# Numerators in three steps over successive slots, another order of the first MLP's first units, and a new spread of the weights' preparation

## The chip, the cores and the metric

The kernel runs on one core of one Trainium2 chip. The metric is the device time of one execution in microseconds. A core has PE (TensorE, matrix products into the PSUM accumulator), VectorE (DVE), ScalarE (ACT), GpSimd (POOL), and SP, which here only issues DMAs. Every engine works through its own queue in program order; the kernel writes that order out by hand, and the engines wait for each other by semaphores.

## The reference

```python
def phi(x):
    proj = np.einsum('bhsd,df->bhsf', x, w_phi)
    proj = proj - np.max(np.abs(proj), axis=-1, keepdims=True)
    return np.concatenate([np.exp(proj), np.exp(-proj)], axis=-1)
q_p, k_p = (phi(q), phi(k))                     # batch 2, heads 8, seq 576, head_dim 64
kv = np.einsum('bhsf,bhsd->bhfd', k_p, v)
z = np.sum(k_p, axis=2)
num = np.einsum('bhsf,bhfd->bhsd', q_p, kv)
den = np.einsum('bhsf,bhf->bhs', q_p, z)[..., None] + 1e-06
x = num / den                                    # as (1152, 512)
...
x = (x @ w_a) * (x @ w_b) @ w_out                # first MLP, d_ff 1536
...
p = domain_probs / (domain_probs.sum(-1, keepdims=True) + 1e-09)
for e in range(4):                               # second MLP, four experts
    out += p[:, e:e + 1] * (np.maximum(x @ w1[e], 0.0) @ w2[e])
```

## The kernel before, in words

**Slots.** Attention runs in slots. Each of 36 items (18 for keys, 18 for queries, `NK = 18`, `NI = 36`) is two tiles of 128 rows of a pair of heads. Slot s projects item s (`pj`: six matmuls, L165 to L167); VectorE takes the row maximum `mx` (L170) and the difference `r` (L172). For a key item ScalarE makes the two exponentials, and three slots later PE adds up `kv`. For a query item PE transposes `r` four slots later (`rt`, L219), and ScalarE writes the exponentials into `qp` (L237). The input of an item is split into a high and a low part three slots ahead, by ScalarE (`xp`, L84) and GpSimd (L85). `pj` and `rt` share four PSUM buffers (pool `u`), so PE can be at most about two slots ahead of VectorE's `r` and ScalarE's `qp`.

**Numerators.** After 4.5 query slots half of a batch's heads is complete, and `num` is called one slot later (for the last half two slots later). `stage_num` issues 48 matmuls on tiles of 32 columns, in three groups of 16 into the two `nd` buffers of PSUM: the denominators (copied out by ScalarE as `den`), then the two halves of the numerator. The third group takes the buffer of the first. In the next slot VectorE makes the reciprocals (`dt`, `rc`, `dt`, `rb`), and in that and the one after multiplies (`x`, L289); a slot after each `x`, `stage_xparts` splits it into `xh` (ScalarE, L295) and `xl` (GpSimd, L296), which the first MLP reads.

**First MLP.** `unit_ab(j, tp)` is for column blocks 2j and 2j+1 (f = 0, 1) and batch `tp`: eight products of 12 matmuls (L608 to L610), four per f, alternating between the a half and the b half of the weights. The product of both, `gg`, is split into `hhb` by ScalarE and VectorE. Eight output products `o1` of six matmuls (L638 to L640) are queued for later; `free_hh(tp)` flushes those that still have to read the part of `hhb` that is about to be written. The first eight products, unit (0, 0), are given out in the last slots (`FILL`), the others by `run`, in the order of the list `order`.

**Preparation of the weights.** Weights arrive as 64-bit numbers in halves (list `f64`: ("ab", 0) with halves 0 and 1, ("ab", 1) with 2 and 3, ("o", 0) with 4 and 5, ("ab", 2) with 6 and 7, ("ab", 3) with 8 and 9, and so on). Each goes through three steps:

```python
def begin(k):   # ScalarE: m (L361), rn (L362)
def middle(k):  # VectorE: m, m, wx (L369, L372, L375); GpSimd: wx (L378); then load_raw() of half k + 2 on SP
def parts(k):   # ScalarE: w (L84); GpSimd: w (L85)
...
for k in range(NW + 2):   # the order of the steps
    if k >= 2: ...parts(k - 2)
    if 1 <= k <= NW: ...middle(k - 1)
    if k < NW: ...begin(k)
```

`prep(n)` does the next n steps; in `run` 1.4 of them fall due after each product, and `need(u)` does at once what a unit still lacks. Half 0 of a block is the a half, half 1 the b half, so the second product of a unit is the first to read the second half. Raw halves of "ab" come in eight DMAs on SP's queue, which also carries the loads of keys, queries (`xraw`) and `v`.

Of the kernel before, what the change touches and what calls it, by code (L numbers as in the profile page):

```python
# [9 lines left out]
F32 = mybir.dt.float32  # L10
F32R = mybir.dt.float32r
U32 = mybir.dt.uint32
AF = mybir.ActivationFunctionType
# [3 lines left out]
B, H, S, D = 2, 8, 576, 64  # L17
# [9 lines left out]
HT = S // 2  # L27
FP1 = FA // 2
# [19 lines left out]
def tile_linear_attention_then_mlps(ctx, tc, qT, kT, v, w_phi, wab, wout, w12, probs, out):  # L48
    nc = tc.nc
# [15 lines left out]
    nd_p = tc.alloc_tile_pool(name="nd", bufs=2, space=PSUM)  # L65
    xt_p = None
    q_p = None
# [6 lines left out]
    with tc.manual_schedule():  # L74
# [80 lines left out]
        kvz_t = {}  # L155
        qp_t = {}
# [56 lines left out]
        def stage_rt(i):  # L213
            kind, b, g, ts_ = items[i]
            r = st_r[i]
            ps = u_p.tile([128, 2, 2, 128], F32, tag="u", name="rt")
            for j in range(2):
                for h in range(2):
                    nc.tensor.transpose(out=ps[:, h, j, :], in_=r[:, 2 * j + h, :], identity=ident)  # L219
            for t in ts_:  # L220
                for p in ([t[0]] if t[0] != "m" else t[1:]):
                    if (b, p) not in qp_t:
                        qp_t[b, p] = q_p.tile([128, 2, 2, S], F32, tag="qp", name="qp", bufs=3)
            done = []
            spans = []
            if ts_[0][0] != "m" and ts_[1][0] == ts_[0][0]:
                spans.append((ts_[0][0], ts_[0][1] * 128, ps.rearrange("p h t s -> p h (t s)"), 256))
            else:
                for j, t in enumerate(ts_):
                    if t[0] == "m":  # L230
                        for m in range(2):
                            spans.append((t[1 + m], 512, ps[:, :, j, 64 * m:64 * m + 64], 64))
                    else:
                        spans.append((t[0], t[1] * 128, ps[:, :, j, :], 128))
            for p, c, src, n in spans:
                for s in range(2):
                    nc.scalar.activation(  # L237
                        out=qp_t[b, p][:, s, :, c:c + n], in_=src, func=AF.Exp, scale=1.0 - 2.0 * s
                    )
            for t in ts_:  # L240
                if t[0] == "m":
                    done.append((b, t[1]))
                elif t[0] % 2 == 1 and t[1] == 3:
                    done.append((b, t[0]))
            return done
# [4 lines left out]
        tt = {}  # L250
        xc = {}

        def stage_num(b, half):
            pairs = [(b, 2 * half + k) for k in range(2)]
            qp = [qp_t.pop(bp) for bp in pairs]
            den = q_p.tile([128, 2, HT], F32, tag="den", name="den", bufs=1)
            x = []
            for k in range(3):
                t = nd_p.tile([128, 2, 512], F32, tag="nd", name="num")
                for i in range(2):  # L260
                    for s in range(2):
                        for n in range(4):
                            h = n % 2
                            c = 64 * (1 - h) if k == 0 else 64 * h + 32 * (k - 1)
                            nc.tensor.matmul(  # L265
                                out=t[32 * n:32 * n + 32, i, 0:HT],
                                lhsT=kvz_t[pairs[n // 2]][:, h, s, c:c + 32],
                                rhs=qp[n // 2][:, s, h, HT * i:HT * i + HT],
                                start=(s == 0), stop=(s == 1), tile_position=(0, 32 * n),
                            )  # L270
                if k == 0:
                    nc.scalar.activation(out=den, in_=t[:, :, 0:HT], func=AF.Copy, bias=1e-6)
                else:
                    x.append(t)
            return x, den

        def stage_rc(den):
            dt = q_p.tile([128, 18, 32], F32, tag="dt", name="dt", bufs=1)
            nc.vector.transpose(out=dt.rearrange("p a b -> p (a b)"), in_=den.rearrange("p a b -> p (a b)"))
            rc = q_p.tile([128, 18, 1], F32, tag="rc", name="rc", bufs=2)  # L280
            nc.vector.reciprocal(out=rc, in_=dt[:, :, 0:1])
            nc.vector.tensor_copy(dt, rc.to_broadcast([128, 18, 32]))
            rb = q_p.tile([128, 2, HT], F32, tag="rb", name="rb", bufs=1)
            nc.vector.transpose(out=rb.rearrange("p a b -> p (a b)"), in_=dt.rearrange("p a b -> p (a b)"))
            return rb

        def stage_x(t, rb):
            x = q_p.tile([128, 2, HT], F32, tag="x", name="x", bufs=2)
            nc.vector.tensor_tensor(out=x, in0=t[:, :, 0:HT], in1=rb, op=ALU.mult)  # L289
            return x  # L290
# [192 lines left out]
        def prep(n):  # L483

            while n > 0 and t_next[0] < len(tasks):
                u, fn, writes = tasks[t_next[0]]
                w = ("load",) + u if writes == "load" else u
                if writes and w in before and uses[before[w]] or t_next[0] >= mark and l_p is None:
                    return
                fn()  # L490
                t_next[0] += 1
                n -= 1
# [8 lines left out]
        pos = [0]  # L501
# [207 lines left out]
        def run(gen, rate, tasks_per):  # L709
# [24 lines left out]
            out=wbp[:, 1], in0=wb.rearrange("p h f -> p (h f)"), in1=wbp[:, 0].bitcast(F32), op=ALU.subtract  # L734
# [14 lines left out]
        NI = len(items)  # L749
        NK = NI // 2  # L750
        todo = {}

        def later(slot, fn, *a):
            todo.setdefault(slot, []).append((fn, a))

        def num(slot, b, half):
            later(slot + 1, div, slot + 1, b, half, *stage_num(b, half))

        def div(slot, b, half, x, den):
            rb = stage_rc(den)  # L760
            for k in range(2):
                later(slot + 1 + k, scaled, slot + 1 + k, b, 2 * half + k, x[k], rb)

        def scaled(slot, b, c, t, rb):
            later(slot + 1, stage_xparts, b, c, stage_x(t, rb))


        FILL = [NI + 4, NI + 6, NI + 7, NI + 8]
        fill = unit_ab(0, 0)

        for slot in range(NI + 10):
            if slot < NI:
                kind, b, g, ts_ = items[slot]
                if slot + 3 < NI:
                    split_x(slot + 3, nc.gpsimd)
                stage_proj(slot)
            if slot == NK + 4:
                for fn, a in todo.pop(slot, []):
                    fn(*a)
                k_p.release()  # L780
                xt_p = tc.alloc_tile_pool(name="xt", bufs=1, side="left", reuse_waits="tile")
                for bb in range(B):
                    xh[bb], xl[bb] = (xt_p.tile([128, KD, S], F32R, tag=f"x{bb}{n}", name="x" + n) for n in "hl")
                q_p = tc.alloc_tile_pool(name="q", bufs=1, side="left", reuse_waits="tile")
            i = slot - 3
            if 0 <= i < NK:
                stage_kv(i)
            i = slot - 4
            if NK <= i < NI:
                for bb, p in stage_rt(i):  # L790
                    if p % 2:
                        n = slot + (2 if i == NI - 1 else 1)
                        later(n, num, n, bb, p // 2)
            for fn, a in todo.pop(slot, []):
                fn(*a)
            if slot == 2:
                for _ in range(2):
                    load_raw()
            if 4 <= slot < 9:
                load_v(1, slot - 4)  # L800
            if slot == 16:
                probabilities()
            if slot in FILL:
                for _ in range(2):
                    next(fill)
                    pos[0] += 1
            if slot in (10, 14):
                prep(3)
            if slot >= NK + 2:
                prep(1)  # L810
        assert not todo
        q_p.release()
        r_p.release()
# [3 lines left out]
        acc_p = ctx.enter_context(tc.tile_pool(name="acc", bufs=4, space=PSUM, reuse_waits="tile"))  # L817


        order = [(j, tp) for j in range(FP1 - 2) for tp in range(B)]  # L820
        order += [(FP1 - 2, 0), (FP1 - 1, 0), (FP1 - 2, 1), None, (FP1 - 1, 1)]
        for jt in order:
            if jt is None:
# [2 lines left out]
            j, tp = jt  # L826
# [63 lines left out]
```

## Time and profile before

| | |
|---|---|
| median of 3 runs | 735.85 us (735.56 to 736.63) |
| the profiled execution | 734.41 us, span 732.6 us |
| PE busy | 711.3 us (97%) |
| VectorE, ScalarE, GpSimd busy | 419.3, 304.2, 302.9 us (57%, 42%, 41%) |
| attention's slots | about 124 us of the span |

A busy PE need not be one at its peak: the records of matmuls overlap, and short gaps hide under their ends. The granted clock of PE is a share of full speed; 1.00 is 2.4 GHz.

### The profile page before, as it was taken

The numbers are of one execution on the slowest core, as the hardware profiler recorded it, in microseconds if no ns is written. First come the engines' busy times: TensorE is split into PE (matmuls) and PEld (weight loads), VectorE is DVE, ScalarE is ACT, GpSimd is POOL, SyncE is SP. The second block draws the span as 40 slices with busy tenths as digits, with TensorE's granted clock in tenths as the row PEclk, the third lists the DMA queues.
The fourth block names the chain that finished last, engine by engine and source line by source line (L and its number), as shares of the span: only waits on it lengthen the run. The fifth ranks groups of instructions, "written<-read, shape, count | busy, mean of one in ns | idle before, by whom it ended". The sixth has DMA issues, their size and how long they took to land.

```text
span 732.6 us, 12645 instructions
## 1 busy us (share of the span) xinstructions
PE 711.3 (97%) x4928; PEld 652.1 (89%) x4928; DVE 419.3 (57%) x717; ACT 304.2 (42%) x626; POOL 302.9 (41%) x277
## 2 busy tenths in 40 slices
PE   7998988999999999999899999999999999999998
PEld 7996657999999999999888898988988898989896
DVE  6678796446666575363545555545455545545454
ACT  6566764554535351243553333323233323333221
POOL 3356545444434354312683425344442535343300
PEclk9999999999999999999999999999999999999999
DMA  7534211222323231022041011111111011100003
GB/s 200 148 111 125 58 59 59 82 92 87 91 83 87 78 96 30 1 58 86 2 116 30 30 57 58 30 55 33 58 40 47 30 59 58 30 29 1 1 1 129
DMA packets 49707, 46.25 MB, mean 63 GB/s; under 512 B 8304, under 2 KB 41584, under 8 KB 49648
## 3 DMA queue, kind: packets, MB, share of 16 engines
q1 hardware_dynamic: 49344, 45.26, 21.0%
q8 instruction: 38, 0.62, 0.4%
q10 hardware_dynamic: 304, 0.20, 0.1%
q14 instruction: 21, 0.17, 0.1%
HBM read 43.08 MB, written 2.36 MB: 62 GB/s over the span
## 4 chain that ended last, share of the span: by engine, by line
PE 92%; DVE 3%; ACT 3%; issue 1%; POOL 1%; DMA 0%; DVEq 0%; ACTq 0%; POOLq 0%
PE acc L682 9%; PE acc L681 9%; PE acc L680 9%; PE ab L609 7%; PE ab L610 7%; PE ab L608 7%; PE X L533 5%; PE kv L199 5%; PE X L534 5%; PE X L535 5%; PE acc L639 3%; PE acc L640 3%; PE acc L638 3%; PE num L265 3%; PE Z L534 2%; PE Z L533 2%
## 5 line engine op out<-in xcount | busy, mean ns | idle before, releaser
L696 DVE SCALAR_TENSOR_TENSOR oacc<-acc,pr,oacc 128x512 f32<-128x512 f32 (+1 forms) x136 | 101.4, 746 | 117.2 <-PE acc L682 117.2
L85 POOL TENSOR_TENSOR w<-wx,w 128x512 fp32r<-128x512 f32 x68 | 92.1, 1355 | 154.9 <-ACT w L84 154.9
L609 PE MATMUL ab<-xl,w 128*128 128x288 f32 x384 | 113.3, 295 | 2.0 <-POOL xl L296 2.0
L85 POOL TENSOR_TENSOR wc<-wt,wc 128x512 fp32r<-128x512 f32 (+1 forms) x48 | 69.8, 1483 | 109.4 <-ACT wc L84 109.4
L682 PE MATMUL acc<-w,hhb 128*128 128x512 f32 x288 | 114.1, 396 | 0.9 <-DVE hhb L657 0.9
L608 PE MATMUL ab<-xh,w 128*128 128x288 f32 x384 | 113.5, 296 | 1.2 <-ACT xh L295 1.2
L610 PE MATMUL ab<-xh,w 128*128 128x288 f32 x384 | 113.4, 295 | 0.0
L681 PE MATMUL acc<-w,hhb 128*128 128x512 f32 x288 | 113.1, 393 | 0.0
L680 PE MATMUL acc<-w,hhb 128*128 128x512 f32 x288 | 112.6, 391 | 0.0
L533 PE MATMUL X<-xc,wc 128*128 128x288 f32 x256 | 77.2, 302 | 1.4 <-ACT h L538 1.4
L534 PE MATMUL X<-xc,wc 128*128 128x288 f32 x256 | 75.8, 296 | 0.7 <-DVE xc L85 0.7
L656 ACT ACTIVATE hhb<-h 128x288 fp32r<-128x288 f32 x64 | 36.2, 566 | 96.8 <-DVE h L541 96.7
L535 PE MATMUL X<-xc,wc 128*128 128x288 f32 x256 | 75.4, 295 | 0.0
L609 PEld LDWEIGHTS ab<-xl,w 128*128 128x128 f32 x384 | 72.2, 188 | 2.2 <-POOL xl L296 2.2
L608 PEld LDWEIGHTS ab<-xh,w 128*128 128x128 f32 x384 | 72.2, 188 | 1.9 <-ACT xh L295 1.5
L378 POOL TENSOR_TENSOR wx<-wx,rn 128x512 uint32<-128x512 uint32 x36 | 46.3, 1287 | 63.1 <-DVE wx L375 63.1
L610 PEld LDWEIGHTS ab<-xh,w 128*128 128x128 f32 x384 | 72.2, 188 | 0.0
L538 ACT ACTIVATE h<-X 128x288 f32<-128x288 f32 x64 | 25.9, 405 | 104.5 <-PE X L535 104.5
L682 PEld LDWEIGHTS acc<-w,hhb 128*128 128x128 f32 x288 | 54.0, 188 | 15.6 <-DVE hhb L657 4.4
L657 DVE SCALAR_TENSOR_TENSOR hhb<-h,hhb 128x288 fp32r<-128x288 f32 x64 | 40.5, 633 | 42.2 <-ACT hhb L656 42.2
L681 PEld LDWEIGHTS acc<-w,hhb 128*128 128x128 f32 x288 | 54.0, 188 | 8.4
L680 PEld LDWEIGHTS acc<-w,hhb 128*128 128x128 f32 x288 | 54.1, 188 | 7.7
(99 smaller groups left out, 1605.8 us busy)
## 6 DMA issues: line engine op xcount, KB each, us to landing
raw<-in_wab SPq DMA_DIRECT2D x192, 64.0 KB, 2.0
wt<-in_w SPq DMA_DIRECT2D x64, 128.0 KB, 2.4
wx<-in_w SPq DMA_DIRECT2D x32, 256.0 KB, 2.9
raw<-in_wout SPq DMA_DIRECT2D x12, 512.0 KB, 3.7
xraw<-in_qT SPq DMA_DIRECT2D x6, 384.0 KB, 3.1
out<-oacc SPq DMA_DIRECT2D x8, 256.0 KB, 2.0
xraw<-in_kT SPq DMA_DIRECT2D x5, 384.0 KB, 4.2
v<-in_v SPq DMA_DIRECT2D x8, 192.0 KB, 4.4
```

The source lines that it names most:

```text
L85: eng.tensor_tensor(out=lo, in0=src, in1=hi.bitcast(F32), op=ALU.subtract)
L378: nc.gpsimd.tensor_tensor(out=x, in0=x, in1=r, op=ALU.add)
L533: nc.tensor.matmul(out=ps, lhsT=whi, rhs=xhi, start=first and a == 0, stop=False, skip_group_check=True)
L534: nc.tensor.matmul(out=ps, lhsT=whi, rhs=xlo, start=False, stop=False, skip_group_check=True)
L535: nc.tensor.matmul(out=ps, lhsT=wlo, rhs=xhi, start=False, stop=a == 1, skip_group_check=True)
L608: nc.tensor.matmul(out=t, lhsT=whi, rhs=hi, start=(c == 0), stop=False)
L609: nc.tensor.matmul(out=t, lhsT=whi, rhs=lo, start=False, stop=False)
L610: nc.tensor.matmul(out=t, lhsT=wlo, rhs=hi, start=False, stop=(c == KD - 1))
L680: nc.tensor.matmul(out=acc, lhsT=hi, rhs=w[:, 0, f], start=f == 0, stop=False)
L681: nc.tensor.matmul(out=acc, lhsT=hi, rhs=w[:, 1, f], start=False, stop=False)
L682: nc.tensor.matmul(out=acc, lhsT=lo, rhs=w[:, 0, f], start=False, stop=f == 1)
L696: nc.vector.scalar_tensor_tensor(out=oc, in0=acc[:, c:c + step], scalar=sc, in1=oc, op0=ALU.mult, op1=ALU.add)
```

## The change

Four things are changed. (1) The numerators are issued in three steps of 16 matmuls in successive slots: denominators (`num`), first half together with the reciprocals (`first`), second half together with the first multiplication (`second`); the second multiplication follows (`third`). The last half is no longer put off by a slot, the loop has one slot less, and `qp` has four buffers. (2) `FILL` gives the eight products of unit (0, 0) out over six slots, from slot 38 on. (3) `PREP` says in which slots a preparation step is made: one in each of the slots 5 to 16, one in 22, 26, 30, 34, one in each of 36 to 44; before, three in slot 10, three in 14, one in each slot from 20 on. (4) Unit (1, 0) goes ahead of (0, 1).

```diff
-                        qp_t[b, p] = q_p.tile([128, 2, 2, S], F32, tag="qp", name="qp", bufs=3)
+                        qp_t[b, p] = q_p.tile([128, 2, 2, S], F32, tag="qp", name="qp", bufs=4)
...
         def num(slot, b, half):
-            later(slot + 1, div, slot + 1, b, half, *stage_num(b, half))
-
-        def div(slot, b, half, x, den):
+            pairs = [(b, 2 * half + k) for k in range(2)]
+            qp = [qp_t.pop(bp) for bp in pairs]
+            kvz = [kvz_t[bp] for bp in pairs]
+            den = stage_den(stage_num(qp, kvz, 0))
+            later(slot + 1, first, slot + 1, b, half, qp, kvz, den)
+
+        def first(slot, b, half, qp, kvz, den):
+            t = stage_num(qp, kvz, 1)
             rb = stage_rc(den)
-            for k in range(2):
-                later(slot + 1 + k, scaled, slot + 1 + k, b, 2 * half + k, x[k], rb)
-
-        def scaled(slot, b, c, t, rb):
-            later(slot + 1, stage_xparts, b, c, stage_x(t, rb))
-
-
-        FILL = [NI + 4, NI + 6, NI + 7, NI + 8]
+            later(slot + 1, second, slot + 1, b, half, qp, kvz, rb, t)
+
+        def second(slot, b, half, qp, kvz, rb, t0):
+            t1 = stage_num(qp, kvz, 2)
+            later(slot + 1, stage_xparts, b, 2 * half, stage_x(t0, rb))
+            later(slot + 1, third, slot + 1, b, half, rb, t1)
+
+        def third(slot, b, half, rb, t1):
+            later(slot + 1, stage_xparts, b, 2 * half + 1, stage_x(t1, rb))
+
+
+        FILL = {NI + 2: 1, NI + 3: 1, NI + 4: 1, NI + 6: 2, NI + 7: 1, NI + 8: 2}
+        PREP = {s: 1 for s in range(5, NK - 1)} | {s: 1 for s in range(NK + 4, NI, 4)} | {s: 1 for s in range(NI, NI + 9)}
...
-                        n = slot + (2 if i == NI - 1 else 1)
-                        later(n, num, n, bb, p // 2)
+                        later(slot + 1, num, slot + 1, bb, p // 2)
...
-            if slot in FILL:
-                for _ in range(2):
-                    next(fill)
-                    pos[0] += 1
-            if slot in (10, 14):
-                prep(3)
-            if slot >= NK + 2:
-                prep(1)
+            for _ in range(FILL.get(slot, 0)):
+                next(fill)
+                pos[0] += 1
+            prep(PREP.get(slot, 0))
...
-        order = [(j, tp) for j in range(FP1 - 2) for tp in range(B)]
+        order = [(0, 0), (1, 0), (0, 1), (1, 1)] + [(j, tp) for j in range(2, FP1 - 2) for tp in range(B)]
```

PE's order in the query slots, at the first numerators (slots 27 and 28). Before:

```order
L219 MATMUL rt<-ident,r 128x128 x4
L265 MATMUL num<-qp,kvz 32x288 x48
L165 MATMUL pj<-wbp,xp 128x256
L166 MATMUL pj<-wbp,xp 128x256
L167 MATMUL pj<-wbp,xp 128x256
L165 MATMUL pj<-wbp,xp 128x256
L166 MATMUL pj<-wbp,xp 128x256
L167 MATMUL pj<-wbp,xp 128x256
L219 MATMUL rt<-ident,r 128x128 x4
```

And of the change:

```order
L219 MATMUL rt<-ident,r 128x128 x4
L260 MATMUL num<-qp,kvz 32x288 x16
L165 MATMUL pj<-wbp,xp 128x256
L166 MATMUL pj<-wbp,xp 128x256
L167 MATMUL pj<-wbp,xp 128x256
L165 MATMUL pj<-wbp,xp 128x256
L166 MATMUL pj<-wbp,xp 128x256
L167 MATMUL pj<-wbp,xp 128x256
L219 MATMUL rt<-ident,r 128x128 x4
L260 MATMUL num<-qp,kvz 32x288 x16
```

The 48 matmuls that stood together are now 16 in this slot, 16 in the next and 16 in the one after; this makes 11 separate bursts in all in place of 4.

ScalarE's order from the last step of unit (0, 0) into the next unit (in the change the rest of unit (1, 0)'s first half). Before, where the next unit is (0, 1):

```order
L538 ACTIVATE hhb<-gg 128x576
L84 ACTIVATE w<-wx 128x512
L295 ACTIVATE xh<-x 128x576
L538 ACTIVATE a<-ab 128x288
L361 ACTIVATE m<-raw 128x512
L362 ACTIVATE rn<-raw 128x512
L538 ACTIVATE part<-acc 128x288 x2
L84 ACTIVATE w<-wx 128x512
```

And of the change, where it is (1, 0); the `w` here is parts 7:

```order
L534 ACTIVATE hhb<-gg 128x576
L84 ACTIVATE w<-wx 128x512
L534 ACTIVATE a<-ab 128x288
L534 ACTIVATE part<-acc 128x288 x2
L357 ACTIVATE m<-raw 128x512
L358 ACTIVATE rn<-raw 128x512
```

Then in the change, at the end of unit (1, 0)'s first half (the first `w` is parts 8, the second parts 9):

```order
L534 ACTIVATE a<-ab 128x288
L534 ACTIVATE part<-acc 128x288
L84 ACTIVATE w<-wx 128x512
L534 ACTIVATE part<-acc 128x288 x5
L534 ACTIVATE hhb<-gg 128x576
L357 ACTIVATE m<-raw 128x512
L358 ACTIVATE rn<-raw 128x512
L84 ACTIVATE w<-wx 128x512
```

The last `xh` of the second batch has moved ahead of this place, and five copies of output products (`part`), which before came one or two at a time, stand ahead of an `hhb` copy and a weight step.

## Rows read from the trace of the kernel before

**Rows 1.** The page, busy time of PE.
```profile
PE 711.3 (97%) x4928; PEld 652.1 (89%) x4928; DVE 419.3 (57%) x717; ACT 304.2 (42%) x626; POOL 302.9 (41%) x277
```

**Rows 2.** Windows: busy PE, PEld, DVE, ACT, POOL; granted clock; DMA share; GB/s.
```profile
30.00:40.00 10.00, 10.00 (x95) 9.74 (x94) 7.47 (x14) 8.00 (x16) 3.55 (x5) 1.00 0.32 88
60.00:70.00 10.00, 6.80 (x69) 5.07 (x71) 9.53 (x15) 9.40 (x26) 8.32 (x9) 1.00 0.48 147
90.00:100.00 10.00, 8.01 (x86) 4.15 (x84) 9.76 (x15) 7.15 (x20) 5.23 (x4) 1.00 0.17 50
130.00:140.00 10.00, 10.00 (x66) 10.00 (x65) 3.35 (x7) 5.38 (x12) 3.51 (x4) 0.83 0.35 105
140.00:150.00 10.00, 10.00 (x78) 10.00 (x77) 5.64 (x10) 5.47 (x12) 5.50 (x4) 1.00 0.29 80
355.00:365.00 10.00, 7.91 (x50) 6.95 (x50) 5.03 (x9) 7.27 (x13) 6.96 (x6) 1.00 0.00 1
```

**Rows 3.** PE's groups up to 135 us: busy, mean ns, idle before and releasers.
```profile
L265 PE MATMUL num<-qp,kvz 128*32 128x288 f32 x384 | 25.8, 408 | 1.3 <-ACT den L272 0.6 <-ACT qp L237 0.5 <-DVE x L289 0.2
L165 PE MATMUL pj<-wbp,xp 128*128 128x256 f32 x72 | 24.2, 337 | 6.4 <-DVE wbp L732 4.4 <-ACT qp L237 1.9
L219 PE MATMUL rt<-ident,r 128*128 128x128 f32 x72 | 10.8, 277 | 3.9 <-ACT qp L237 2.9 <-DVE r L172 0.9
```

**Rows 4.** Timeline of PE: start, duration (us), instruction, in brackets idle before.
```profile
68.12 6.03 PE L265 MATMUL num<-qp,kvz 128*32 128x288 f32 x96
74.08 0.39 PE L165 MATMUL pj<-wbp,xp 128*128 128x256 f32 x1
...
75.25 0.36 PE L165 MATMUL pj<-wbp,xp 128*128 128x256 f32 x1
...
76.66 0.35 PE L165 MATMUL pj<-wbp,xp 128*128 128x256 f32 x1
...
79.32 0.39 PE L165 MATMUL pj<-wbp,xp 128*128 128x256 f32 x1 [1.27 <-ACT qp L237]
...
100.65 2.15 PE L265 MATMUL num<-qp,kvz 128*32 128x288 f32 x32 [0.60 <-ACT den L272]
...
126.11 0.40 PE L608 MATMUL ab<-xh,w 128*128 128x288 f32 x1 [1.25 <-ACT xh L295]
128.47 0.40 PE L609 MATMUL ab<-xl,w 128*128 128x288 f32 x1 [1.97 <-POOL xl L296]
```

**Rows 5.** Timeline of VectorE in query slots 22 to 26.
```profile
58.33 0.42 DVE L369 TENSOR_SCALAR m<-m 128x512 f32<-128x512 f32 x1
...
59.91 0.68 DVE L170 TENSOR_REDUCE mx<-pj 128x4 f32<-128x512 f32 x1
...
64.02 0.91 DVE L369 TENSOR_SCALAR m<-m 128x512 f32<-128x512 f32 x1
...
66.09 0.68 DVE L170 TENSOR_REDUCE mx<-pj 128x4 f32<-128x512 f32 x1
```

**Rows 6.** Timeline of ScalarE, one begin step in slot 23.
```profile
59.11 0.66 ACT L361 ACTIVATE m<-raw 128x512 f32<-128x512 f32 x1
...
60.23 0.41 ACT L84 ACTIVATE xp<-xraw 128x256 fp32r<-128x256 f32 x1
```

**Rows 7.** Timeline at the end of unit (0, 0) and after it, three engines.
```profile
123.79 0.46 DVE L615 TENSOR_TENSOR gg<-ab,a 128x288 f32<-128x288 f32 x1 [1.11 <-PE ab L610]
...
124.28 0.68 ACT L538 ACTIVATE hhb<-gg 128x576 fp32r<-128x576 f32 x1 [1.62 <-DVE gg L615]
124.87 0.61 ACT L84 ACTIVATE w<-wx 128x512 fp32r<-128x512 f32 x1
...
125.56 1.32 POOL L85 TENSOR_TENSOR w<-wx,w 128x512 fp32r<-128x512 f32 x1 [1.69 <-ACT w L84]
...
133.74 0.41 ACT L538 ACTIVATE part<-acc 128x288 f32<-128x288 f32 x1 [0.82 <-PE acc L640]
```

**Rows 8.** Timeline of SP: eight DMAs of one raw half.
```profile
33.68 3.88 SPq L339 DMA_DIRECT2D raw<-in_wab  x8
```

More of the change, by code (lines that the diff above doesn't have):

```diff
@@ L251, in tile_linear_attention_then_mlps, with stage_num, stage_den @@
         xc = {}
-        def stage_num(b, half):
-            pairs = [(b, 2 * half + k) for k in range(2)]
-            qp = [qp_t.pop(bp) for bp in pairs]
-            den = q_p.tile([128, 2, HT], F32, tag="den", name="den", bufs=1)
[L257 to L275, printed above, removed]
+        def stage_num(qp, kvz, k):
+            t = nd_p.tile([128, 2, 512], F32, tag="nd", name="num")
+            for i in range(2):
+                for s in range(2):
+                    for n in range(4):
+                        h = n % 2
+                        c = 64 * (1 - h) if k == 0 else 64 * h + 32 * (k - 1)
+                        nc.tensor.matmul(
+                            out=t[32 * n:32 * n + 32, i, 0:HT],
+                            lhsT=kvz[n // 2][:, h, s, c:c + 32],
+                            rhs=qp[n // 2][:, s, h, HT * i:HT * i + HT],
+                            start=(s == 0), stop=(s == 1), tile_position=(0, 32 * n),
+                        )
+            return t
+        def stage_den(t):
+            den = q_p.tile([128, 2, HT], F32, tag="den", name="den", bufs=1)
+            nc.scalar.activation(out=den, in_=t[:, :, 0:HT], func=AF.Copy, bias=1e-6)
+            return den
         def stage_rc(den):
@@ L756, in num @@
         def num(slot, b, half):
-            later(slot + 1, div, slot + 1, b, half, *stage_num(b, half))
-        def div(slot, b, half, x, den):
-            rb = stage_rc(den)
-            for k in range(2):
-                later(slot + 1 + k, scaled, slot + 1 + k, b, 2 * half + k, x[k], rb)
-        def scaled(slot, b, c, t, rb):
-            later(slot + 1, stage_xparts, b, c, stage_x(t, rb))
-        FILL = [NI + 4, NI + 6, NI + 7, NI + 8]
+            pairs = [(b, 2 * half + k) for k in range(2)]
[5 more added lines that the diff above has]
+            t = stage_num(qp, kvz, 1)
+            rb = stage_rc(den)
+            later(slot + 1, second, slot + 1, b, half, qp, kvz, rb, t)
[7 more added lines that the diff above has]
+        PREP = {s: 1 for s in range(5, NK - 1)} | {s: 1 for s in range(NK + 4, NI, 4)} | {s: 1 for s in range(NI, NI + 9)}
         fill = unit_ab(0, 0)
-        for slot in range(NI + 10):
+        for slot in range(NI + 9):
             if slot < NI:
```

## The prediction

> **What bounds the kernel now.** I read the page first, then the windows, then PE's own groups and its timeline, then the queues of the engines that PE waits for. The page has PE busy 97% of the span [rows 1], so only PE's 21.3 us of idle time, and time that a busy record hides, can be won. The windows say where. In 30 to 40 us (the key slots) PE is busy 10.00 of 10 while VectorE is at 7.47 and ScalarE at 8.00, although three preparation steps lie in that stretch; in the query slots PE falls to 6.80 and 8.01 while VectorE stands at 9.53 and 9.76 [rows 2]. By PE's groups its waits up to 135 us are: transposes `rt` 2.9 us on ScalarE's `qp` and 0.9 on VectorE's `r`, projections `pj` 1.9 on `qp`, numerators 1.3 [rows 3]. The timeline adds two waits at the start of the second batch's first unit, 1.25 us on `xh` and 1.97 on `xl` [rows 4], and the windows show what followed them: a granted clock of 0.83 over 130 to 140 us (part of it at 1.2 GHz), 66 matmuls where the next ten microseconds hold 78 [rows 2]. So the bound is VectorE and ScalarE in the query slots, a latency chain at the end of attention, and PE everywhere else.
>
> **Up to the first numerators.** Before, slots 22 to 26 carry the steps of three weight halves. On VectorE one middle step takes the queue from 58.33 to 59.91 (1.58 us), another from 64.02 to 66.09 (2.07) [rows 5]. On ScalarE a begin step takes from 59.11 to 60.23 (1.12) [rows 6]. After, these slots hold one parts step at 22 and one middle at 26, the latter behind the work that the first numerators wait for. So VectorE loses 3.6 us ahead of them, and ScalarE two begins and one copy, 2 x 1.12 + 0.6 = 2.8. Both queues pace PE here, so the smaller counts: 2.8 us, about the 2.9 that `rt` waited.
>
> **From there to the end of the fill.** Three things go. The wait of 1.27 us on `qp` at 79.32 [rows 4], and the waits around the third numerators (0.9 on `r`, 1.3 in the group itself [rows 3]): 3.5 together. And a hidden one: a `pj` and `rt` pair takes 1.17 us when nothing holds it (74.08 to 75.25) and 1.41 when VectorE sets the pace (75.25 to 76.66 [rows 4]). With a numerator step in nine of the slots PE has work of its own there; some ten pairs by 0.24 is 2.4. Two things come. One burst of 96 records takes 6.03 us, one of 32 takes 2.15 [rows 4], so each further burst costs (3 x 2.15 - 6.03)/2 = 0.21; the order has 11 bursts in place of 4: 7 x 0.21 = 1.5. And the third batch of numerators starts one slot row behind `qp` again: its transposes come straight ahead of it, and ScalarE has an `xh` and a weight copy in between (0.7 + 0.6): 1.3. Net 3.5 + 2.4 - 1.5 - 1.3 = 3.1. Bounds: if the waits only move, the 5.9 falls away and the costs stay, -2.8; if none is left, 5.9 - 1.5 = 4.4. I take 3.1, since in the order each VectorE chain (transposes, reciprocal) now stands a slot ahead of its reader.
>
> The Trainium skill ("TensorEngine Tiling (Array Packing)", Key Properties) says that changing the tiling mode drains TensorE, which speaks against splitting bursts of 32-column matmuls among full-width ones. The rows show such a toll; the page gives no price.
>
> **The second batch's first unit.** Unit (1, 0) now stands ahead of (0, 1). It brings 8 products of 12 matmuls and the 8 output products of unit (0, 0), 6 matmuls each: 144 by 0.128 us (78 in ten microseconds [rows 2]) is 18.4 us in which the last `xh` and `xl` are made. The 3.2 us of waits go, and with them the slow clock, 12 matmuls by 0.128 = 1.5. Gain 4.7.
>
> **What the later weights cost.** The steps fall from 32 to 25 by the end of the slots, so the second halves of the weights ("ab", 2) and ("ab", 3) (steps parts 7 and parts 9) are issued just ahead of their readers. ScalarE's order has parts 7 right behind the `hhb` copy of unit (0, 0). In the trace that chain runs: `gg` 123.79, `hhb` 124.28, `w` copy 124.87 for 0.61, GpSimd's `w` 125.56 for 1.32 [rows 7]. Counted from `gg`, the copy is done at +1.69 and the difference at +3.09. PE's second product is due at about +1.2 and reads the difference with its third matmul: waits of 0.5 and 1.1, 1.6 us. Parts 9 is worse: ScalarE must first copy the last of five output products that are flushed (133.74 is such a copy, 0.31 to the next), then `hhb` 0.6, a begin 1.1, then `w` 0.61, and GpSimd 1.32. The second product is due 1.3 us after that last copy starts, the weight at 2.6 and its difference at 4.0: waits of 1.3 and 1.1, 2.4 us. Together 4.0. Bounds: 0, if PE is late by as much; and, with parts 11 as a third, each with a whole middle ahead of it (1.58 + 1.3 + 0.6 + 1.3 = 4.8), 14.4. I take 4.0, since the rows of the chain are those of this very place.
>
> Such waits can bring the slow clock again. The 3.2 us within 4 us at 124.9 did; about 2.1 us idle in 355 to 365 left it at 1.00 [rows 2]. Parts 9 lies between: 0 or 1.5 us, I take 0.75.
>
> **Edits at nothing.** Six more steps in key slots 5 to 16: ScalarE 6 x 0.57 us, VectorE 6 x 0.5, GpSimd 6 x 0.9, over some 30 us in which PE does not wait though three steps stood together [rows 2]. Their DMAs: eight pieces of a raw half keep SP for 3.9 us (33.68 [rows 8]); they now stand ahead of the last `v` rows and one key chunk, which the readers need two slots (some 5 us) later. If that cover fails, each microsecond is PE's. The fourth `qp` buffer lets transposes start sooner and costs no instruction. From the first MLP's last units on the order is the same on all engines.
>
> **Sum.** 2.8 + 3.1 + 4.7 - 4.0 - 0.75 = 5.85 us off the profiled execution's 734.41: 728.6. The median of the runs lies 1.4 above that execution, so I predict 735.85 - 5.85 = 730.0.
>
> **Rivals.**
> - *The late weights hide.* If ScalarE and GpSimd get the two parts steps done in time (both are below half busy around there), the 4.75 come back: 725.2. For it: GpSimd idles over a microsecond ahead of its weights' steps [rows 7]. Against: the chain is one of latency, not load. 0.15.
> - *The query slots only shift their waits.* VectorE still has some 10.5 us per half batch against PE's 11.5, so a slowed step makes it the bound again. Then the second term is -2.8 and the whole gain 0: 735.9, no change. For it: VectorE's 9.76 at 90 to 100 us. Against: 12 of 20 steps leave these slots. 0.12.
> - *Dearer bursts.* The 0.21 us may be paid again on entering each burst, between `pj`, `rt` and `ab` as neighbours; 7 x 0.21 = 1.5 more, and the median comes to 731.5, inside the forecast's range. For it: no row has a burst of 32 among full-width matmuls. Against: the bursts of 32 that were measured began after a wait, and carry their entry. 0.08. The Trainium skill's rule above, a drain at each change of mode, is this mechanism.
> - *Slower: weights in series.* Parts 7, 9 and 11 each pay the whole chain, 14.4, and each brings the slow clock, 4.5. That is 18.9 against gains of 10.6: 744. It decides from 10.6 us of such waits. For it: each begin needs a raw half whose buffer the middle before it frees. Against: after the slots, GpSimd needs 2.6 us per half and gets three steps in about 3.5 us. 0.06.
> - *The change does not act*: the order of weights forces the same waits elsewhere, 735.9. 0.03.
>
> **Chances.** The forecast (727.5 to 733) has 0.56. About 0.2% (1.5 us) is what a measurement of this kernel can tell from no change. Faster by more: 0.56 + 0.15 + 0.08 and half of the second rival's spread, 0.84; same 0.09; slower 0.07. The range of 8 in 10 reaches from the first rival to just short of no change: 725.0 to 734.6.
>
> **What would show it.** Right: PE's first numerators near 65.3 us, the second near 76, the fill's end near 117 against 123.5; no wait on `xl` at the second batch; two PE waits on GpSimd's `w` in unit (1, 0), at its second and sixth product, 1.6 and 2.4 us. Wrong, if the key slots show PE waits, if VectorE is still above 9.5 in the query slots, or if waits on `w` come in more than three places.

## The result and the profile after

The changed kernel takes 729.34 us in the median (727.97 to 729.87), the kernel before beside it 735.70 (735.11 to 736.63): a ratio of 0.991, 95% interval 0.9892 to 0.9927. The profiled execution takes 727.97 us with a span of 726.2, against 734.41 and 732.6.

The page of the changed kernel, its line of busy times ([rows 1] is the one of before):

```profile
PE 709.9 (98%) x4928; PEld 650.3 (90%) x4928; DVE 424.1 (58%) x717; ACT 303.1 (42%) x626; POOL 304.2 (42%) x277
```

The windows answer to [rows 2]:

```profile
60.00:70.00 10.00, 9.87 (x103) 7.26 (x105) 9.33 (x16) 8.75 (x29) 6.71 (x8) 1.00 0.37 110
90.00:100.00 10.00, 10.00 (x119) 6.61 (x108) 7.60 (x10) 7.72 (x21) 5.44 (x5) 1.00 0.18 55
130.00:140.00 10.00, 7.53 (x55) 7.07 (x54) 5.17 (x8) 5.31 (x11) 4.33 (x3) 1.00 0.18 54
```

PE is full in the query slots (9.87 and 10.00 where it was 6.80 and 8.01), and VectorE is off its limit at 90 to 100 us. At 130 to 140 us the clock holds at 1.00, but PE is idle a quarter of the time. The table of PE's waits (what waited for what: us in total, times, longest) says for whom:

```profile
PE pj L165 <- DVE wbp L728: 4.4, 1, 4.4
PE ab L606 <- POOL w L85: 2.2, 2, 1.3
PE ab L604 <- ACT w L84: 1.4, 2, 1.1
...
PE acc L636 <- POOL w L85: 1.0, 1, 1.0
...
PE rt L219 <- ACT qp L237: 0.5, 1, 0.5
```

The waits on `qp`, `den`, `r`, `xh` and `xl` of [rows 3, 4] are gone but for one of 0.5. In their place stand weights, `w`. (The rows left out belong to the second MLP, and the kernel before has them too.) PE's timeline says where:

```profile
65.34 2.15 PE L260 MATMUL num<-qp,kvz 128*32 128x288 f32 x32
...
118.02 0.40 PE L604 MATMUL ab<-xh,w 128*128 128x288 f32 x1 [0.28 <-ACT w L84]
...
119.42 0.40 PE L606 MATMUL ab<-xh,w 128*128 128x288 f32 x1 [0.87 <-POOL w L85]
...
131.87 0.29 PE L606 MATMUL ab<-xh,w 128*128 128x288 f32 x1
133.30 0.40 PE L604 MATMUL ab<-xh,w 128*128 128x288 f32 x1 [1.15 <-ACT w L84]
133.54 0.29 PE L605 MATMUL ab<-xl,w 128*128 128x288 f32 x1
135.16 0.40 PE L606 MATMUL ab<-xh,w 128*128 128x288 f32 x1 [1.33 <-POOL w L85]
...
144.78 0.40 PE L636 MATMUL acc<-hhb,w 128*128 128x288 f32 x1 [1.01 <-POOL w L85]
```

The first numerators start at 65.34 instead of 68.12, with PE's first matmul at 4.38 in both. The last `gg` of unit (0, 0) comes at 116.27 instead of 123.79 [rows 7], so 7.5 us are won up to there. The second MLP starts at 339.89 instead of 346.41 (ScalarE's first `oacc`), so 1.0 of them is lost again in between.

### The profile page after: what moved, and what is told of

Its sections match the earlier page's. It is cut to its first block, busy times and chain, and to the rows that moved or that the text cites. A ratio compares the mean times of both kernels' runs of the same rounds, so it can differ in the third digit from the quotient of the medians.

```text
span 726.2 us, 12646 instructions
## 1 busy us (share of the span) xinstructions
PE 709.9 (98%) x4928; PEld 650.3 (90%) x4928; DVE 424.1 (58%) x717; ACT 303.1 (42%) x626; POOL 304.2 (42%) x277
## 4 chain that ended last, share of the span: by engine, by line
PE 95%; ACT 2%; DVE 1%; POOL 1%; issue 1%; DMA 0%; DVEq 0%; ACTq 0%; POOLq 0%
PE acc L678 9%; PE acc L677 9%; PE acc L676 9%; PE ab L606 7%; PE ab L604 7%; PE ab L605 7%; PE X L529 5%; PE kv L199 5%; PE X L530 5%; PE X L531 5%; PE acc L635 3%; PE num L260 3%; PE acc L636 3%; PE acc L634 3%; PE Z L529 2%; PE Z L530 2%
## 5 line engine op out<-in xcount | busy, mean ns | idle before, releaser
L374 POOL TENSOR_TENSOR wx<-wx,rn 128x512 uint32<-128x512 uint32 x36 | 46.4, 1290 | 50.9 <-DVE wx L371 50.9
```

The lines of the kernel that those rows point to most:

```text
L374: nc.gpsimd.tensor_tensor(out=x, in0=x, in1=r, op=ALU.add)
```

## The experiments

The kernels ran in three groups, each beside the kernel before; its medians were 734.99, 735.91 and 735.70 us. Medians of one kernel wander by about 1 us, and PE's first matmul starts between 4.4 and 5.5 us from profile to profile; where starts in two traces are compared, that start is taken off. From there to the first `rt` the traces differ by up to 1.3 us more (51.8 to 53.1), so lengths inside one trace are the safer comparison.

### First: the parts alone, and the order of units

**The kernel before with the order alone.**

```diff
-        order = [(j, tp) for j in range(FP1 - 2) for tp in range(B)]
+        order = [(0, 0), (1, 0), (0, 1), (1, 1)] + [(j, tp) for j in range(2, FP1 - 2) for tp in range(B)]
```

> The kernel before with unit (1, 0) ahead of (0, 1) and nothing else. My account: the waits of 1.25 and 1.97 us on xh and xl go, and with them the slow clock (1.5 us) and two restarts (0.5); weights are early here (32 steps), so no new wait: 735.7 - 5.2 = 730.5. Rival (the gain of the change comes from the slots alone, the order only moves the wait): 735.7.

733.74 us, ratio 0.9973 (0.9962 to 0.9985): between the two. The waits on `xh` and `xl` are gone, but a new one stands in their place. ScalarE's and PE's timelines:

```profile
135.70 0.67 ACT L361 ACTIVATE m<-raw 128x512 f32<-128x512 f32 x1 [3.04 <-DMA raw<-in_wab]
...
137.27 0.40 PE L638 MATMUL acc<-hhb,w 128*128 128x288 f32 x1 [1.19 <-ACT part L538]
```

A begin step waits 3.04 us for its raw half, and the copies of output products behind it in ScalarE's queue hold PE's accumulators.

**The kernel before with the new spread alone.** The diff is the `PREP` of the change, put into the kernel before.

> The kernel before with the new spread of the preparation and nothing else. My account: the 2.8 us ahead of the first numerators and about 1 us of VectorE's pacing behind them; the waits on xh and xl and the slow clock stay, and weights are in time since (0, 1) comes first: 735.7 - 4 = 731.7. Rival (the spread is the whole gain of the slots, the split of the numerators nothing): 735.7 - 7.5 = 728.2. Rival (the split is the whole gain): 735.7.

732.56 us, ratio 0.9944 (0.9922 to 0.9966). The waits of 1.2 and 2.0 on `xh` and `xl` are still there. PE's timeline, at the first `rt` and the first numerators:

```profile
57.31 0.60 PE L219 MATMUL rt<-ident,r 128*128 128x128 f32 x4
...
65.13 6.03 PE L265 MATMUL num<-qp,kvz 128*32 128x288 f32 x96
```

From the one to the other it takes 7.82 us; in the kernel before 10.67 (57.45 to 68.12), in the changed kernel 7.82 (57.52 to 65.34).

**The changed kernel with the order of before** (the diff of the first experiment, the other way round).

> The changed kernel with the order of units of before, (0, 1) ahead of (1, 0). My account: the waits on late weights go (6.5 us with the clock), since parts 7, 9 and 11 have a unit more time; the last xl now ends at 117.6 and would be read at about 117.0, so a wait of some 1 us comes back: 723.8. Rival (the wait on xh and xl comes back whole, with the slow clock, 5.2): 728.

722.98 us, ratio 0.982 (0.9802 to 0.9838), 6 us better than the change. From 60 to 345 us PE has no wait but the 0.5 on `qp`. The timelines of VectorE, ScalarE, GpSimd and PE at the end of the fill:

```profile
107.02 0.76 DVE L285 TENSOR_TENSOR x<-num,rb 128x576 f32<-128x576 f32 x1 [0.41 <-PE num L260]
...
114.14 0.75 DVE L285 TENSOR_TENSOR x<-num,rb 128x576 f32<-128x576 f32 x1
...
114.92 0.69 ACT L291 ACTIVATE xh<-x 128x576 fp32r<-128x576 f32 x1 [0.49 <-DVE x L285]
...
115.56 2.81 POOL L292 TENSOR_TENSOR xl<-x,xh 128x576 fp32r<-128x576 f32 x2
...
117.09 0.46 DVE L611 TENSOR_TENSOR gg<-ab,a 128x288 f32<-128x288 f32 x1 [1.84 <-PE ab L606]
...
118.00 0.29 PE L604 MATMUL ab<-xh,w 128*128 128x288 f32 x1
118.43 0.40 PE L605 MATMUL ab<-xl,w 128*128 128x288 f32 x1
```

Of the last half's two multiplications one starts 10 us ahead of the fill's last `gg` and the other 3, and PE loses 0.30 us on `xl` (0.43 from start to start, where 0.13 is usual). In the kernel before, VectorE had the reciprocals at 114.3 (113.53 + 0.78), but both multiplications stood behind a product of the fill and a middle step in its queue; ScalarE then had the last `xh` behind the fill's last `hhb` and a weight copy ([rows 7]):

```profile
113.53 0.78 DVE L284 STREAM_TRANSPOSE rb<-dt 128x576 f32<-128x576 f32 x1
...
118.64 0.76 DVE L621 TENSOR_TENSOR hhb<-gg,hhb 128x576 fp32r<-128x576 f32 x1 [0.75 <-ACT hhb L538]
...
120.28 0.69 DVE L375 SCALAR_TENSOR_TENSOR wx<-raw,m 128x512 uint32<-128x512 uint32 x1
120.89 0.75 DVE L289 TENSOR_TENSOR x<-num,rb 128x576 f32<-128x576 f32 x1
...
121.92 0.75 DVE L289 TENSOR_TENSOR x<-num,rb 128x576 f32<-128x576 f32 x1
...
125.39 0.67 ACT L295 ACTIVATE xh<-x 128x576 fp32r<-128x576 f32 x1
```

That `xh` starts 2.7 us after its `x` is done (121.92 + 0.75); in the run with the old order it starts right behind its `x` (114.14 + 0.75), ahead of the fill's last `gg` and of the `hhb` behind it. So the swap of units is not needed against these waits, and it is dear.

**The changed kernel with seven preparation steps more by the end of the slots.**

```diff
-        PREP = ... | {s: 1 for s in range(NI, NI + 9)}
+        PREP = ... | {s: 1 if s < NI + 2 else 2 for s in range(NI, NI + 9)}
```

> The changed kernel with two preparation steps in each of slots 38 to 44, so that 32 are done before unit (1, 0), as before. My account: the five waits on late weights (4.6 us of idle time, 5.8 with the restarts) go, and the slow clock that follows them in most runs (about 1): 729.3 - 6.5 = 722.8. Rival (the extra steps push the copies and splits of the last slots back, so the fill ends later by as much): 728 to 729.5.

726.57 us, ratio 0.9877 (0.9856 to 0.9897). No wait on `w` is left, but 2.32 us at 130.32 us on a `part` copy behind a begin that waits 2.92 for its raw half, as in the first experiment. So the late weights were the wait, but curing them this way made another.

### Second: what the split, the spread and the fourth buffer bring

All three have the order of before.

**Split, slot less and fill, without the new spread.**

```diff
-        PREP = {s: 1 for s in range(5, NK - 1)} | {s: 1 for s in range(NK + 4, NI, 4)} | {s: 1 for s in range(NI, NI + 9)}
+        PREP = {10: 3, 14: 3} | {s: 1 for s in range(NK + 2, NI + 9)}
```

> The changed kernel with the old order of units and the old spread of the weights' steps; the split numerators, the slot less, the fill and the fourth qp buffer stay. My account as it now stands: the waits on xh and xl go through the earlier numerators and the slot less, so they stay away here; what comes back is VectorE's pace ahead of the first numerators (first numerators again near 68 us) and part of the waits after it. With the second run of this study (only the spread, 3.2 us better than before) and the changed kernel with the old order (12.8 better than before in the same call's terms) this should be 3 to 4 us above the latter: about 726.5. Rival: the spread is what brings the xh and xl of the last half forward, and without it the waits of 1.2 and 2.0 us and the lower clock return: about 732.

726.94 us, ratio 0.9877 (0.9855 to 0.9898), as expected. PE waits 3.0 us on `qp` ahead of the first numerators again, which start at 68.47; there is no wait on `xh` or `xl`.

**Numerators in one burst.** The three calls of `stage_num` stand together in `num`; the rest of `first`, `second` and `third` stays in its slots.

```diff
+            t = [stage_num(qp, kvz, k) for k in (1, 2)]
...
-            t = stage_num(qp, kvz, 1)
...
-            t1 = stage_num(qp, kvz, 2)
```

> The changed kernel with the old order of units, but with all three numerator groups in the num slot, as before; the multiplications stay in the same slots. My account: PE then waits again for the den copy inside the burst and runs dry around it (0.6 us per burst, and pj and rt pairs at VectorE's pace after it), while seven separate bursts and their toll of 0.21 us each go: 2 to 3 us above the changed kernel with the old order, about 725.5. Rival: splitting only moves the same matmuls about, and the slot less and the spread do it all: the same time as the changed kernel with the old order, about 723, or less by the 1.5 us of toll.

726.98 us, ratio 0.9885 (0.9864 to 0.9907): 4 us worse than the split, more than expected. PE's timeline:

```profile
63.67 0.60 PE L219 MATMUL rt<-ident,r 128*128 128x128 f32 x4
64.20 6.03 PE L260 MATMUL num<-qp,kvz 128*32 128x288 f32 x96
...
70.97 0.60 PE L219 MATMUL rt<-ident,r 128*128 128x128 f32 x4
...
77.20 6.08 PE L260 MATMUL num<-qp,kvz 128*32 128x288 f32 x96 [0.99 <-DVE x L285]
```

The second burst waits until VectorE has emptied an `nd` buffer; seven waits of 2.6 us in all stand here between 70 and 120 us where the split has hardly one. By the traces, it takes 53.6 us from the first numerators to the last `gg` of unit (0, 0) (64.20 to 117.80), with the split 50.9 (65.34 to 116.27): 2.7 of the 4 us lie there.

**Three `qp` buffers** (`bufs=3` for `bufs=4`).

> The changed kernel with the old order of units and three qp buffers instead of four. My account: a half's qp is now read until the third numerator step, two slots later than before, so ScalarE's exponentials of the next half wait for that step and PE's transposes wait behind them: 1 us for each of the first three halves, about 726. Rival: the exponentials come late enough anyway, and the fourth buffer is worth nothing: about 723.

723.07 us, ratio 0.9832 (0.9815 to 0.9849): my account was wrong, the fourth buffer is worth nothing that shows.

**The changed kernel itself** in the same group.

> The changed kernel as it is, beside the three others on one chip. If the swap of units costs what the run with the old order showed, this lies near 729, some 6 us above the changed kernel with the old order; if that difference came from the runs' scatter, nearer 725.

729.72 us, ratio 0.9921 (0.9904 to 0.9937): 6.65 us above the run with three buffers and the old order.

### Third: the slot less, the fill, and a last try for the swap

**The last half put off by a slot again** (order of before).

```diff
-                        later(slot + 1, num, slot + 1, bb, p // 2)
+                        n = slot + (2 if i == NI - 1 else 1)
+                        later(n, num, n, bb, p // 2)
...
-        for slot in range(NI + 9):
+        for slot in range(NI + 10):
```

> The changed kernel with the old order of units, and the numerators of the last half put off by a slot again (and the slot more that this needs); split, spread, fill stay. If the slot less is what brings the last xh and xl in time, they are now late: they were ready 0.3 us after PE wanted them, and a slot of the fill holds one or two products of 1.55 us, so PE waits some 1.5 to 3 us, with or without the lower clock behind it (1.5): 725 to 727, I say 726. Rival: the split alone does it, since the chain is shorter: 723, as with the slot less.

727.40 us, ratio 0.9898 (0.988 to 0.9916). PE's timeline and the window:

```profile
117.91 0.40 PE L604 MATMUL ab<-xh,w 128*128 128x288 f32 x1 [0.79 <-ACT xh L291]
120.28 0.50 PE L605 MATMUL ab<-xl,w 128*128 128x288 f32 x1 [1.97 <-POOL xl L292]
```
```profile
120.00:130.00 10.00, 9.72 (x61) 9.72 (x62) 3.58 (x7) 3.71 (x8) 2.54 (x3) 0.83 0.26 62
```

The waits are back, the lower clock (part of the window at 1.2 GHz) with them. In this setting the slot less is worth about 4 us.

**The slot less alone, in the kernel before** (the same lines the other way round).

> The kernel before with one thing of the change: the last half's numerators are not put off by a slot, and the loop has one slot less; everything else as before. My account: the multiplication of the last half stands in VectorE's order one slot further ahead of the fill's products, xh and xl come in time, the waits of 1.2 and 2.0 us and the lower clock behind them go: 735.9 - 4.7 = 731.2. Rival: the put-off covered ScalarE's last qp, and PE now waits there for it, or VectorE's chain ends as late as before: 734 to 736.

733.98 us, ratio 0.998 (0.997 to 0.9991): 1.7 of the 4.7 that I had expected. The wait on `xh` is gone and 0.6 is left on `xl`, but PE now waits at the last numerators:

```profile
105.49 0.68 PE L265 MATMUL num<-qp,kvz 128*32 128x288 f32 x4 [1.71 <-DVE x L289]
107.40 6.02 PE L265 MATMUL num<-qp,kvz 128*32 128x288 f32 x92 [1.23 <-ACT qp L237]
```

The put-off had kept a single burst clear of VectorE's `x` and ScalarE's last `qp`. With the split, the first step needs one free buffer and the others come slots later; only then does the slot less pay in full. By the traces, from the last `gg` of unit (0, 0) to the first `oacc` it takes 218.2 us where the kernel before takes 222.6, but from the first numerators to that `gg` 58.8 instead of 55.7.

**The changed kernel with its own order and two steps more**, in slots 40 and 42.

```diff
-        PREP = ... | {s: 1 for s in range(NI, NI + 9)}
+        PREP = ... | {s: 2 if s in (NI + 4, NI + 6) else 1 for s in range(NI, NI + 9)}
```

> The changed kernel with its own order of units and two preparation steps in place of one in slots 40 and 42, so that the steps late by a little come two steps sooner and no begin step stands in the flush of output products. If the swap costs only through late weights and the begin in the flush, those waits go and the time is that of the old order: 723. Rival: the flush of five products itself, or the weights of the unit after it, keep a part of the cost: 726 or more.

727.26 us, ratio 0.9886 (0.9872 to 0.9901); the rival held. Unit (1, 0) has its weights in time and no begin step stands between the flushed copies, yet the rows of five queues show a chain:

```profile
129.69 0.76 DVE L617 TENSOR_TENSOR hhb<-gg,hhb 128x576 fp32r<-128x576 f32 x1 [4.47 <-ACT hhb L534]
...
132.10 1.28 POOL L374 TENSOR_TENSOR wx<-wx,rn 128x512 uint32<-128x512 uint32 x1 [5.61 <-DVE wx L371]
...
132.10 15.38 SPq L335 DMA_DIRECT2D raw<-in_wab  x24
...
138.59 0.66 ACT L357 ACTIVATE m<-raw 128x512 f32<-128x512 f32 x1 [4.24 <-DMA raw<-in_wab]
...
140.94 0.40 PE L634 MATMUL acc<-hhb,w 128*128 128x288 f32 x1 [2.38 <-ACT w L84]
```

ScalarE copies five flushed products before it makes `hhb`. VectorE waits for that `hhb` 4.47 us, with a middle step of the weights behind it; the loads of the next raw halves are issued behind that step, ScalarE's begin waits for them, and PE for the weight behind the begin. PE loses 2.38 us, then 0.72 on GpSimd's `w`, and the granted clock over 140 to 145 us is 0.82.

**The fill of before** in the changed kernel with the old order (`FILL = {NI + 4: 2, NI + 6: 2, NI + 7: 2, NI + 8: 2}`).

> The changed kernel with the old order of units and the old fill (two products each in slots 40, 42, 43, 44). My account: PE loses the products that covered the last transposes in slots 38 and 39, and waits there for ScalarE's qp and VectorE's r about 1.5 us: 724.5. Rival: the products are as well placed later, where they cover the reciprocals: 723.

723.50 us, ratio 0.9833 (0.982 to 0.9846): the spread of the fill is worth 0.5 us at most, with one wait of 0.39 us at the last numerators.

## Why the prediction was right, and which step of it was wrong

The time came out at 729.3 against 730.0, but one step gave the credit to the wrong edit. That the sum held so closely is partly luck: two terms were off by 1.6 and 1.0 us in opposite directions, and the wrong edit and the right ones are all in the change, so the number could not tell them apart. The predicted terms and what the two profiled executions give (in us):

| term | predicted | measured | how measured |
|---|---|---|---|
| up to the first numerators | -2.8 | -2.8 | 68.12 to 65.34 |
| from there to the last `gg` of unit (0, 0) | -3.1 | -4.7 | 7.52 less 2.78 |
| the second batch's waits and the clock behind them | -4.7 | -4.7 | from that `gg` to `oacc`: 222.62 before, 217.91 with the old order |
| late weights, with the clock behind them | +4.75 | +5.7 | the same stretch: 223.62 after, 217.91 with the old order |
| sum | -5.85 | -6.5 | `oacc` 346.41 to 339.89 |

**First numerators: right, and by the cause given.** With the old spread the 3.0 us on `qp` come back and the numerators start at 68.47; less the starts of PE, the difference to the changed kernel is 63.78 - 60.96 = 2.8. The spread alone, in the kernel before, shortens the way from the first `rt` to the first numerators by as much (10.67 to 7.82). The medians put the spread at 3.9; the trace with the old spread also has the lower clock at the second MLP (388.1 us from the first `oacc` to the end instead of 386.3), and its runs scatter from 723.99 to 728.24. The second batch's numerators start at 76.77 (76 predicted).

**To the end of the fill: right in kind, mis-sized by 1.6.** The 1.3 us that I charged for the third numerators standing close behind `qp` did not come: no wait stands at them. What is left, 4.4 by the upper bound, is nearly the 4.7 measured. The split is not the whole of it. With one burst and all else as in the change, but the old order of units, the stretch takes 53.6 us, 2.7 more than with the split; the kernel before takes 55.7. So the other edits bring 2.1 of the 4.7; the spread alone, in the kernel before, takes the stretch to 53.3 (65.13 to 118.44).

The toll of a burst is larger than I took, since I left out what it costs to enter one. PE's timeline in the changed kernel, a slot with a burst and one without:

```profile
71.66 0.60 PE L219 MATMUL rt<-ident,r 128*128 128x128 f32 x4
72.19 2.15 PE L260 MATMUL num<-qp,kvz 128*32 128x288 f32 x32
...
75.09 0.60 PE L219 MATMUL rt<-ident,r 128*128 128x128 f32 x4
...
76.24 0.60 PE L219 MATMUL rt<-ident,r 128*128 128x128 f32 x4
```

From `rt` to `rt` it takes 3.43 us with the burst and 1.15 without, so 32 records add 2.28. In the one-burst run 96 records add 70.97 - 63.67 - 1.15 = 6.15. Each further burst therefore costs (3 x 2.28 - 6.15)/2 = 0.34, where the prediction had 0.21: seven are 2.4 us, hidden in a gain twice as large. A part of the toll lies ahead of the burst: 0.53 us from the start of `rt` to the burst, but 0.35 from `rt` to `pj` where no burst stands between (75.09 to 75.44). So the 4.4 came near the 4.7 only because the time that was to be won, 5.9 in the prediction, was too small as well: 4.7 and 2.4 make 7.1. The Trainium skill ("TensorEngine Tiling (Array Packing)", Key Properties) says that a change of tiling mode drains TensorE. These rows agree that entering and leaving costs something; they show no more than that, and the run with one burst was still the slower by 4 us.

**The second batch's first unit: right size, wrong edit.** "The 3.2 us of waits go, and with them the slow clock" holds, but the prediction said it of unit (1, 0) standing ahead of (0, 1), and the changed kernel with the old order shows that the waits go without that. The swap can remove them, as it does in the kernel before; there it is not needed twice. What I missed is that the split and the slot less bring each of the last half's two multiplications ahead of one more `gg` in VectorE's queue, and the last `xh` ahead of the fill's last `hhb` and a weight copy in ScalarE's. ScalarE's order, printed ahead of the prediction, shows that this `xh` has moved; I drew nothing from it. I had costed the slot less at nothing of its own. It is neither edit alone: the slot less alone gives 1.7 us, the split with the put-off leaves 3 us of waits, both together leave 0.3.

**What the later weights cost: right mechanism, right places, a little too small.** At parts 7 PE is idle 0.28 + 0.87 = 1.15 (1.6 predicted), at parts 9 1.15 + 1.33 = 2.48 (2.4), and 1.01 more at an output product, which I had no term for. ScalarE's timeline in the changed kernel is the chain of the prediction:

```profile
130.62 0.41 ACT L534 ACTIVATE part<-acc 128x288 f32<-128x288 f32 x1 [0.39 <-PE acc L636]
130.92 0.68 ACT L534 ACTIVATE hhb<-gg 128x576 fp32r<-128x576 f32 x1
131.50 0.67 ACT L357 ACTIVATE m<-raw 128x512 f32<-128x512 f32 x1
132.06 0.66 ACT L358 ACTIVATE rn<-raw 128x512 uint32<-128x512 uint32 x1
132.64 0.61 ACT L84 ACTIVATE w<-wx 128x512 fp32r<-128x512 f32 x1
```

The idle records add up to 4.6 and the stretch is 5.7 longer. The rows show the rest as PE's restart. From 131.87 to 133.30 it takes 1.43 us; 1.15 are idle and 0.13 is usual, so 0.15 to 0.16 is lost beside the record, and the next matmul (133.54) starts 0.24 later instead of 0.13. That is 0.26 at each of the five waits, 1.3 in all and 5.9 with the idle time; the stretch is only 5.7 longer because the run with the old order loses a few tenths of its own, 0.4 of them at `xl`. The prediction had no term for the restart. Its term for the clock (0.75) is not borne out in the profiled execution, where the clock fell at none of these places: 4.0 us of waits were predicted and 5.7 came. In the other three runs the mean granted clock was 0.997 or 0.998 instead of 1.000, and they took 1.2 to 1.9 us longer; where it fell in them, no trace shows. The price is not one of the numbers in `PREP` alone: 7 steps more gave 726.57, two more 727.26, and each time a wait came up elsewhere on the same chain of copies, middle steps and raw loads. Whether some other spread makes the swap free was not tried further; the old order makes it needless.

**Rivals.** The late weights did not hide. The query slots did not only shift their waits: VectorE is at 7.60 of 10 at 90 to 100 us. It is still near its limit earlier, at 9.55 in 50 to 60 us, where PE keeps its one wait of 0.5 on `qp`, and at 9.33 in 60 to 70, where PE is full. The dearer bursts are borne out in part: 0.34 each, between my 0.21 and the rival's 0.42. The weights did not come in the long series, though there was a third place, at an output product. The edits costed at nothing held, but for the slot less: in 30 to 40 us PE is at 10.00 of 10 although six steps more lie in the key slots and VectorE rises to 9.36, and the fourth `qp` buffer and the spread of the fill are worth less than the runs can tell.

By medians: the split with the slot less brings about 9.0 us, the spread 3.9 more, and the swap gives 6.7 back. The changed kernel without the swap, at 723, is the best of all that ran.

## What to carry to other kernels

When an edit in a change removes a wait, ask which of the other edits removes it too: a gain has to be counted at the last edit that is needed for it, and an edit that is no longer needed keeps its price. Where a result is late, look at where its instruction stands in its engine's queue and not only at when its inputs are ready; here a multiplication started 6.6 us after its reciprocals were done, and a copy in ScalarE's queue 2.7 us after its input was. A step that waits for a load, put ahead of short copies in the same queue, holds up everything that those copies free.

## What the runs showed of the hardware that was not expected

- The granted clock does not follow from the waits alone. At the start of the second MLP the same two waits (0.69 or 0.70 us, then 1.39 to 1.41) stand in all fourteen profiled executions, some 12 and 15 us after ScalarE's first `oacc`, and the order of instructions from that `oacc` on is the same. In nine of them the clock stays at 1.00 there and the rest of the program takes 386.2 to 386.4 us; in five it falls (to 0.70 to 0.83 over 5 us) and the rest takes 387.6 to 388.2. The kernel before is one of the nine, and the prediction took its 2.1 idle us at this place as a case that leaves the clock alone. The windows of one of the five, the changed kernel with the old order, and of one of the nine, the run with three `qp` buffers:

```profile
350.00:355.00 5.00, 5.00 (x29) 4.95 (x29) 1.18 (x4) 3.44 (x8) 4.60 (x4) 0.73 0.00 0
```
```profile
350.00:355.00 5.00, 5.00 (x40) 4.96 (x39) 1.82 (x5) 4.24 (x11) 4.76 (x4) 1.00 0.01 2
```

  The window holds 29 matmuls instead of 40; 11 at 0.125 us (40 in 5 us) are 1.4 us, and the runs of one kernel lie that far apart and more (728.52 to 731.12 for the changed kernel in its second group). The Trainium skill ("TensorE: Matmul & The Clock Gate", Part 1) says that the number of slow matmuls at a kernel's start differs from run to run; these traces show such a difference in the middle of a program.
- A wait of 2.32 us at 130 us left the clock at 1.00 in the run with seven steps more; waits of 0.79 and 1.97, the second ending at 120.28 us, were followed by a lower one in the run with the last half put off. The changed kernel's 1.15 and 1.33 at 133 and 135 us left it at 1.00.
- A wait of PE costs more than its idle record: 0.26 us more at each of the five waits on `w`, 0.16 before the matmul that waited and 0.10 before the next.
